# Attention kernel: the order of TensorE's instructions written out by hand, the other engines left to the scheduler

## The chip, the cores and the metric

The kernel runs on one core of a Trainium2 chip. The core has TensorE (PE, with its weight loads as PEld), VectorE (DVE), ScalarE (ACT), GpSimd (POOL) and a queue of transfers (SP); each works through its own instructions in order, and semaphores tie them together. The metric is the time of one execution in microseconds. Matmuls read on-chip memory (SBUF) and write accumulators (PSUM).

## The reference, cut to what matters

An attention whose mask allows only queries and keys of one cluster, followed by two expert layers. The attention, the part that changes:

```
B, H, S, D = 2, 8, 768, 64          # 16 heads, 16 clusters of each
q_assign = argmax(q_n @ c_n.T);  k_assign = argmax(k_n @ c_n.T)
mask = q_assign[:, :, :, None] == k_assign[:, :, None, :]
scores = where(mask, scale * q @ k.T, -1e9)
attn = softmax(scores);  out = attn @ v
...
x = moe(x)       # 1536 rows, 8 experts, with a skip
x = moe2(x)      # the same with an output gate
```

## The kernel before

**A head in six steps.** The 16 heads (`t`) are taken one after the other, and each in six steps (`i`) of 128 queries. `score` makes the 128x768 scores of a step in PSUM with four products: two with K and Q split in a high and a low part (`KA`, `QA`, 512 and 256 columns), two with `KB` and `QB` (L475, L477), whose last 16 rows hold the one-hot cluster of each token, so that the mask is added by the product. DVE takes the row maximum (`mx`, L481), ACT the exp with its sum (`probs`, L486). `flips` turns the 128x768 probabilities with six transpositions (L493) into two PSUM tiles `tp` of three each, which ACT and DVE copy to `PT`. There are two buffers for the scores, and two for `tp`. The code of a step first issues the score of the step after it, then the transpositions of its own.

**The products with V.** After three steps a half of the head (384 queries) is complete, and `av` multiplies it with V: six products (k = 0 to 5) of 64 x 384, the even ones into the upper 64 rows of one PSUM tile, the odd ones into the lower. In the trace each of them is two instructions (L505). `merge` then divides by the sums and multiplies with `G` (unit matrix and gate weights, L520).

**The work ahead.** In steps 3 to 5 of head `t`, `dots` makes the cluster products of head `t + 2`, four at a time, in the free quarter of the first `tp` tile of the step (L421); `dots_sum` adds them up on DVE (`dt`, L428), which frees that tile. Before L428 reads the tile, ACT must have copied its other part. `cluster` finds the cluster on DVE, `one_hot` transposes the result (L455, two products a head), and three transfers on SP bring it through memory into rows 64 to 79 of `QB` and `KB`. `load` and `split` fetch and split Q and K three and two heads ahead; `split` runs on POOL. In heads 1 to 8, `split_weights` splits a piece of expert weights, the high part on ACT (L136), the low part on DVE (L139); `behind` puts it behind the step's maximum and exp. From head 8 on `bg` runs the routing of the first batch a few instructions a step, its placing products at L263.

**What sets the order.** Through the attention the language's scheduler sets the order of each engine's instructions: it takes the program's order as a priority, and moves what it holds ready earlier. From the experts on, `tc.manual_schedule()` makes every engine issue in the order in which the code is written. There `tokens` runs the first expert's products with a list of events between them, which also finishes the last head.

Of the kernel before, what the change touches and what calls it, by code (L numbers as in the profile page):

```python
# [23 lines left out]
B, H, S, D = 2, 8, 768, 64  # L24
# [3 lines left out]
NJ = S // 128  # L28
# [12 lines left out]
def fused_kernel(ctx: ExitStack, tc: tile.TileContext, qT, kT, v, cN, wg, w11, w12, w21, w22, out):  # L41
# [17 lines left out]
    def iota_f(pool, name, n, pattern, base, cm):  # L59
        ti = pool.tile([128, n], I32, name=name + "i")  # L60
        nc.gpsimd.iota(ti, pattern=pattern, base=base, channel_multiplier=cm)
        tf = const.tile([128, n], F32, name=name)
        nc.gpsimd.tensor_copy(out=tf, in_=ti)
        return tf
# [102 lines left out]
    bg = Background()  # L167
# [163 lines left out]
    def route1(L, b, ps, pool, after=None, slack=6):  # L331
        do = pool.tile([128, NJ], F32, tag="do", name="do")
        nc.vector.tensor_scalar(out=do, in0=L[:, :, E], scalar1=0.0, scalar2=None, op0=ALU.is_gt)
        yield
        yield from route(L[:, :, 0:E], None, tok1[:, NJ * b:NJ * b + NJ], do, NJ, base1, TB1, ps, pool, after, slack)
# [23 lines left out]
    asm = pool("asm", 1, actx)  # L359
# [16 lines left out]
    def load(t):  # L376
        if t >= NH:
            return
        b, h = heads[t]
        qp = ld.tile([128, S], F32, tag="qp", name="qp")  # L380
        kp = ld.tile([128, S], F32, tag="kp", name="kp")
        vp = vpb.tile([128, NJ, D], F32, tag="vp", name="vp")
        for dst, src in ((kp, kT), (qp, qT)):
            for p in (LO, HI):
                nc.sync.dma_start(out=dst[p], in_=src[b, h])
        nc.sync.dma_start(out=vp, in_=v[b, :, h])
        raw[t] = (qp, kp, vp)

    def split(t):

        if t >= NH:
            return
        qp, kp, vp = raw.pop(t)
        QA = spl.tile([128, S], F32R, tag="QA", name="QA")
        KA = spl.tile([128, S], F32R, tag="KA", name="KA")
        QB = spl.tile([80, S], F32R, tag="QB", name="QB")
        KB = spl.tile([80, S], F32R, tag="KB", name="KB")
        if t == 0:
            nc.scalar.copy(out=KA[:], in_=kp)
            nc.vector.tensor_tensor(out=KA[HI], in0=kp[HI], in1=as32(KA[HI]), op=ALU.subtract)  # L400
            nc.scalar.activation(out=QA[:], in_=qp, func=AF.Copy, scale=SCALE)
            nc.vector.scalar_tensor_tensor(out=QA[LO], in0=qp[LO], scalar=SCALE, in1=as32(QA[LO]), op0=ALU.mult, op1=ALU.subtract)  # L402
        else:
            nc.gpsimd.tensor_scalar(out=KA[:], in0=kp, scalar1=1.0, scalar2=1.0, op0=ALU.mult, op1=ALU.mult)
            nc.gpsimd.tensor_tensor(out=KA[HI], in0=kp[HI], in1=as32(KA[HI]), op=ALU.subtract)
            nc.gpsimd.tensor_scalar(out=QA[:], in0=qp, scalar1=SCALE, scalar2=1.0, op0=ALU.mult, op1=ALU.mult)
            nc.gpsimd.tensor_scalar(out=qp[LO], in0=qp[LO], scalar1=SCALE, scalar2=1.0, op0=ALU.mult, op1=ALU.mult)
            nc.gpsimd.tensor_tensor(out=QA[LO], in0=qp[LO], in1=as32(QA[LO]), op=ALU.subtract)
        nc.sync.dma_start(out=as32(QB[LO]), in_=as32(QA[HI]))
        nc.sync.dma_start(out=as32(KB[LO]), in_=as32(KA[LO]))  # L410
        ops[t] = (QA, KA, QB, KB, vp)
# [18 lines left out]
    def cluster(t, n):  # L430
        if t >= NH:
            return
        for _ in range(n):
            next(clus[t][0])
# [60 lines left out]

    avp = {}

    def av(t, half, PT, k0, k1):
        vp = ops[t][4]
        if k0 == 0:  # L500
            avp[t] = ps_o.tile([128, 384], F32, tag="o", name="o")
        po = avp[t]
        for k in range(k0, k1):
            r = 64 * (k % 2)
            nc.tensor.matmul(out=po[r:r + 64, :], lhsT=vp[:, k, :], rhs=PT[:, k, :], start=(k < 2), stop=(k >= NJ - 2))  # L505
        if k1 == NJ:
            ot = asm.tile([128, 384], F32, tag="ot", name="ot", bufs=2)
            nc.scalar.copy(out=ot, in_=po)
            avp[t] = ot

    def merge(t, half):
        b, h = heads[t]
        ot = avp.pop(t)
        j0 = 3 * half
        rr = asm.tile([128, 3], F32, tag="rr", name="rr", bufs=2)
        nc.scalar.activation(out=rr, in_=sums[t][:, j0:j0 + 3], func=AF.Copy, bias=1e-9)
        nc.vector.reciprocal(out=rr, in_=rr)
        pf = ps_m.tile([128, 3, D + NG], F32, tag="misc", name="pf")
        for j in range(3):
            nc.tensor.matmul(out=pf[:, j], lhsT=ot[:, 128 * j:128 * j + 128], rhs=G[:, h], start=True, stop=True)  # L520
        if b not in xb:
            xb[b] = xp.tile([128, NJ, DM], F32, tag="xb", name="xb")
            lg[b] = (xp if b == 0 else const).tile([128, NJ, NG], F32, name=f"lg{b}")
        rb = rr.unsqueeze(2)
        x, L = xb[b][:, j0:j0 + 3], lg[b][:, j0:j0 + 3]
        if h == 0:
            nc.vector.tensor_tensor(out=L, in0=pf[:, :, D:], in1=rb.to_broadcast([128, 3, NG]), op=ALU.mult)
        else:
            lt = asm.tile([128, 3, NG], F32, tag="lt", name="lt", bufs=2)
            nc.vector.tensor_tensor(out=lt, in0=pf[:, :, D:], in1=rb.to_broadcast([128, 3, NG]), op=ALU.mult)  # L530
            (nc.vector if t == NH - 1 else nc.gpsimd).tensor_tensor(out=L, in0=L, in1=lt, op=ALU.add)
        nc.vector.tensor_tensor(out=x[:, :, D * h:D * h + D], in0=pf[:, :, 0:D], in1=rb.to_broadcast([128, 3, D]), op=ALU.mult)
        if h == H - 1:
            r0 = S * b + 384 * half
            for dst in (X, X2):
                nc.sync.dma_start(out=dst[r0:r0 + 384, :].rearrange("(j p) d -> p j d", p=128), in_=x)
# [43 lines left out]
    nc.vector.tensor_tensor(out=chl[:, :, 1], in0=c3, in1=as32(chl[:, :, 0]), op=ALU.subtract)  # L580

    split(0)
    d16 = iota_f(asm, "d16", NCL, [[-1, NCL]], NCL, 0)
    for c in (2, 1, 0):
        dp = ps_t.tile([128, 4, 128], F32, tag="tp", name="dp0")[:, 0].rearrange("p (t s) -> p t s", t=4)
        dots(0, c, dp)
        dots_sum(0, c, dp)
# [7 lines left out]
        nc.sync.dma_start(out=G[p, :, D:], in_=wg.rearrange("(h d) g -> d h g", d=D))  # L595
        nc.gpsimd.tensor_scalar(out=G[p, :, 0:D], in0=ident[p, p].unsqueeze(1).to_broadcast([64, H, D]), scalar1=1.0, scalar2=1.0, op0=ALU.mult, op1=ALU.mult)
    io128, io12, d8, tok1 = late_constants(asm)
    load(1)
    split(1)
    load(2)  # L600

    wsets = [w_tiles(wA, "A"), None]
    wdone = 0
    def flips(t, i, pr, hook=None, after=None):
# [15 lines left out]
    for c in range(3):  # L620
        dp = ps_t.tile([128, 4, 128], F32, tag="tp", name="dp1")[:, 0].rearrange("p (t s) -> p t s", t=4)
        dots(1, c, dp)
        dots_sum(1, c, dp)
    PT = {}
    for g, (t, i) in enumerate(steps[:-1]):
        half = i // 3
        if i % 3 == 0:
            PT[t, half] = ptb.tile([128, NJ, 384], F32, tag="PT", name="PT")
        old = pr
        cur = score(*steps[g + 1])  # L630
        pr = probs(*steps[g + 1], *cur)
        if i == 0:
            load(t + 3)
            split(t + 2)
            cluster(t + 1, 2)
        elif i == 1:
            if t:
                av(t - 1, 1, PT[t - 1, 1], 0, 6)
            cluster(t + 1, 2)
        elif i == 2:  # L640
            if t == NH - 1:
                first_turn()
            if t:
                merge(t - 1, 1)
                if t == H:
                    bg.add(route1(lg[0], 0, ps_m, asm, None, 2))
                    bg.add(first_tile())
                    bg.add(route_skip(lg[0], tok1[:, 0:NJ], ps_m, asm, 2))
            cluster(t + 1, 1)
            one_hot(t + 1)  # L650
        elif i == 3:
            if 1 <= t <= 8:
                if t == 1:
                    fetch(False, 2)
                behind(lambda: split_weights(t - 1, False, False))
        elif i == 4:
            behind(flush_late)
            av(t, 0, PT[t, 0], 0, 6)
        elif i == 5:
            merge(t, 0)  # L660

        dp = []

        def hook(tp):
            if i > 2 and t + 2 < NH:
                dp.append(tp[:, 3].rearrange("p (t s) -> p t s", t=4))
                dots(t + 2, i - 3, dp[0])

        def after(tp):
            if dp:  # L670
                dots_sum(t + 2, i - 3, dp[0])

        flips(t, i, old, hook, after)
        behind(lambda: bg.step(2))
    bg.drain()
    tl = NH - 1

# [375 lines left out]
    def first_of_batch1(L):  # L1053
# [29 lines left out]
    ht = h_tiles(128)  # L1083
    xg[0, 0] = rows_in(X[0:S], gi1[:, 0, 0:1])
    py = tokens(first, wsets[0], ht, half_of(0), events(
        (0, lambda: merge(tl, 0)), (18, last_probs), (26, lambda: av(tl, 1, PT[tl, 1], 0, 2)), (30, lambda: av(tl, 1, PT[tl, 1], 2, 6)),
        (36, last_merge), *plan(P['E0']), *steps(P['q4'], 72, 1)), (38, 43, 48, 54))
    flush()
    close_first(0, 0, 0, py)
# [209 lines left out]
```

## Time and profile before

| | us |
|---|---|
| median of 3 runs | 734.42 |
| lowest, highest | 728.52, 736.29 |
| the profiled execution | 733.56 |
| its span, first to last instruction | 731.8 |
| PE busy | 664.9 (91%) |
| DVE, ACT, POOL busy | 462.4, 401.2, 190.7 |
[...]

The attention ends, and the first expert product (L725) begins, at 314.75 us of the span; the rest belongs to the two expert layers. Starts of PE's instructions in a timeline tell its pace better than durations, since neighbouring matmuls overlap.

### The profile page before, as it was taken

The numbers are of one execution on the slowest core, as the hardware profiler recorded it, in microseconds if no ns is written. First come the engines' busy times: TensorE is split into PE (matmuls) and PEld (weight loads), VectorE is DVE, ScalarE is ACT, GpSimd is POOL, SyncE is SP. The second block draws the span as 40 slices with busy tenths as digits, with TensorE's granted clock in tenths as the row PEclk, the third lists the DMA queues.
The fourth block names the chain that finished last, engine by engine and source line by source line (L and its number), as shares of the span: only waits on it lengthen the run. The fifth ranks groups of instructions, "written<-read, shape, count | busy, mean of one in ns | idle before, by whom it ended". The sixth has DMA issues, their size and how long they took to land. (4 is left out here: it accounts for less than half of the span.)

```text
span 731.8 us, 11917 instructions
## 1 busy us (share of the span) xinstructions
PE 664.9 (91%) x4196; PEld 526.5 (72%) x4196; DVE 462.4 (63%) x964; ACT 401.2 (55%) x801; POOL 190.7 (26%) x193
## 2 busy tenths in 40 slices
PE   3889999999999999988888889789996999999995
PEld 2667666666667666767777778668885888899784
DVE  4546666667776676538768688657855755665620
ACT  2547666666565666644646666536634655555420
POOL 4614444444334330005202112202132022103011
PEclk9989999999999999998999899999999999999998
DMA  6665655556533110085737688637643576657200
GB/s 160 148 158 117 142 116 116 116 116 209 131 88 101 33 34 12 12 299 194 251 127 274 195 290 278 207 115 256 226 138 116 188 262 240 215 193 237 72 7 29
DMA packets 53034, 113.72 MB, mean 155 GB/s; under 512 B 7938, under 2 KB 15746, under 8 KB 52928
## 3 DMA queue, kind: packets, MB, share of 16 engines
q1 hardware_dynamic: 48016, 98.56, 44.8%
q0 software_dynamic: 4912, 13.88, 5.9%
q8 instruction: 51, 0.84, 0.5%
q14 instruction: 55, 0.45, 0.2%
HBM read 93.52 MB, written 14.71 MB: 148 GB/s over the span
## 5 line engine op out<-in xcount | busy, mean ns | idle before, releaser
L486 ACT ACTIVATE pr<-s,mx 128x768 f32<-128x768 f32 x96 | 86.8, 904 | 48.2 <-DVE mx L481 46.7
L481 DVE TENSOR_REDUCE mx<-s 128x1 f32<-128x768 f32 x96 | 90.9, 954 | 35.1 <-PE s L477 32.6
L493 PE MATMUL tp<-ident,pr 128*128 128x128 f32 x576 | 96.3, 291 | 2.9 <-ACT pr L486 2.7
L505 PE MATMUL o<-PT,vp 128*64 128x384 f32 x384 | 93.1, 499 | 0.6
L611 ACT COPY PT<-tp 128x384 f32<-128x384 f32 x144 | 67.0, 481 | 47.2 <-PE tp L493 28.5
L493 PEld LDWEIGHTS tp<-ident,pr 128*128 128x128 f32 x576 | 66.0, 146 | 35.9 <-ACT pr L486 12.5
L701 POOL DMA_INDIRECT xg<-x_rows,gi x33 | 40.2, 1217 | 112.2 <-PEq L1154 37.8
L475 PE MATMUL s<-KA,QA 128*128 128x512 f32 x192 | 64.8, 404 | 4.7 <-DVE QA L402 3.1
L725 PE MATMUL ph<-w1hA,xt 128*128 128x256 f32 x208 | 52.0, 313 | 8.7 <-DVEq L1154 5.2
L477 PE MATMUL s<-KB,QB 80*128 80x512 f32 x192 | 54.5, 369 | 1.1 <-ACT KB L445 1.1
L505 PEld LDWEIGHTS o<-PT,vp 128*64 128x64 f32 x384 | 29.8, 136 | 35.4 <-issue 30.4
L725 PE MATMUL ph<-w1hB,xt 128*128 128x256 f32 x192 | 46.2, 312 | 9.3 <-PEq L1154 4.2
L725 PE MATMUL py<-w2hA,hh 128*128 128x512 f32 x112 | 47.5, 424 | 4.1 <-DVE hh L799 4.1
L725 PE MATMUL py<-w2hB,hh 128*128 128x512 f32 x112 | 46.6, 417 | 3.5 <-DVE hh L799 3.5
L725 PEld LDWEIGHTS ph<-w1hA,xt 128*128 128x128 f32 x208 | 38.6, 204 | 12.8 <-issue 10.9
L725 PE MATMUL py<-w2lA,hh 128*128 128x512 f32 x112 | 47.1, 420 | 0.0
L725 PE MATMUL py<-w2lB,hh 128*128 128x512 f32 x112 | 46.3, 413 | 0.0
L613 DVE COPY PT<-tp 128x384 f32<-128x384 f32 x48 | 26.8, 557 | 29.1 <-PE tp L493 27.8
L725 PEld LDWEIGHTS ph<-w1hB,xt 128*128 128x128 f32 x192 | 35.5, 208 | 11.8 <-issue 10.2
L837 DVE SCALAR_TENSOR_TENSOR hl<-phw,hh 128x256 fp32r<-128x256 f32 x48 | 20.2, 421 | 36.0 <-ACT hh L836 36.0
L139 DVE TENSOR_TENSOR w1lA<-raw,w1hA 128x1024 fp32r<-128x1024 f32 x32 | 39.8, 1257 | 2.8 <-ACT w1hA L136 2.7
L136 ACT CAST w1hA<-raw 128x1024 fp32r<-128x1024 f32 x32 | 33.0, 1045 | 14.2 <-PEq L1154 6.2
(240 smaller groups left out, 1643.3 us busy)
## 6 DMA issues: line engine op xcount, KB each, us to landing
raw<-w SPq DMA_DIRECT2D x128, 512.0 KB, 4.9
kp<-kT SPq DMA_DIRECT2D x32, 192.0 KB, 4.6
qp<-qT SPq DMA_DIRECT2D x32, 192.0 KB, 4.6
x_rows<-xb SPq DMA_DIRECT2D x8, 768.0 KB, 5.7
vp<-v SPq DMA_DIRECT2D x16, 192.0 KB, 3.8
KB<-KA SPq DMA_DIRECT2D x16, 192.0 KB, 3.6
QB<-QA SPq DMA_DIRECT2D x16, 192.0 KB, 3.4
one_hot<-st SPq DMA_DIRECT2D x15, 96.0 KB, 1.7
```

Of the source, the lines that this page charges most:

```text
L136: nc.scalar.copy(out=hi, in_=src)
L139: nc.vector.tensor_tensor(out=lo, in0=src, in1=as32(hi), op=ALU.subtract)
L475: nc.tensor.matmul(out=s[:, n0:n1], lhsT=QA[:, sl], rhs=KA[:, n0:n1], start=True, stop=False)
L477: nc.tensor.matmul(out=s[:, n0:n1], lhsT=QB[:, sl], rhs=KB[:, n0:n1], start=False, stop=True)
L481: paced["DVE"] = nc.vector.tensor_reduce(out=mx, in_=s, axis=AX.X, op=ALU.max, negate=True).ins
L486: paced["ACT"] = nc.scalar.activation(out=pr, in_=s, func=AF.Exp, bias=mx, accum_out=sums[t][:, i:i + 1]).ins
L493: nc.tensor.transpose(out=tp[:, kk], in_=pr[:, 128 * k:128 * k + 128], identity=ident)
L505: nc.tensor.matmul(out=po[r:r + 64, :], lhsT=vp[:, k, :], rhs=PT[:, k, :], start=(k < 2), stop=(k >= NJ - 2))
L611: nc.scalar.copy(out=dst, in_=tp[:, 0:3])
L613: nc.vector.tensor_copy(out=dst, in_=tp[:, 0:3])
L701: nc.gpsimd.indirect_dma_start(out=xg, out_offset=None, in_=src, in_offset=bass.IndirectOffsetOnAxis(ap=gi, axis=0))
L725: nc.tensor.matmul(**kw)
```

## The change

PE alone is taken out of the scheduler's hands for the loop over heads: `tc.manual_schedule(engines={PE})`. The loop's body is written in the order wanted of PE: the score of the next step, then the six products of a half (in steps 0 and 3), the transpositions with the dots, and then the merge (after steps 1 and 4) or the one-hot pair (after step 2). The products of a head's second half move from step 1 of the next head to its step 0, those of the first half from step 4 to step 3. The merge of the last head's first half stands in the loop instead of in the experts' events. Ahead of the loop, the loads of heads 1 and 2 and the split of head 1 stand earlier. The number of instructions is the same.

```diff
     split(0)
+    load(1)
+    split(1)
     d16 = iota_f(asm, "d16", NCL, [[-1, NCL]], NCL, 0)
+    load(2)
...
-    load(1)
-    split(1)
-    load(2)
...
+    order = ExitStack()
+    order.enter_context(tc.manual_schedule(engines={mybir.EngineType.PE}))
     for g, (t, i) in enumerate(steps[:-1]):
...
         if i == 0:
+            if t:
+                av(t - 1, 1, PT[t - 1, 1], 0, 6)
             load(t + 3)
             split(t + 2)
-            cluster(t + 1, 2)
+            cluster(t + 1, 3)
         elif i == 1:
-            if t:
-                av(t - 1, 1, PT[t - 1, 1], 0, 6)
             cluster(t + 1, 2)
         elif i == 2:
             if t == NH - 1:
                 first_turn()
+        elif i == 3:
+            av(t, 0, PT[t, 0], 0, 6)
+            if 1 <= t <= 8:
...
+        elif i == 4:
+            behind(flush_late)
...
+        flips(t, i, old, hook, after)
+        if i == 1:
             if t:
                 merge(t - 1, 1)
...
-            cluster(t + 1, 1)
+        elif i == 2:
             one_hot(t + 1)
-        elif i == 3:
...
         elif i == 4:
-            behind(flush_late)
-            av(t, 0, PT[t, 0], 0, 6)
-        elif i == 5:
             merge(t, 0)
...
-        flips(t, i, old, hook, after)
         behind(lambda: bg.step(2))
+    order.close()
...
     py = tokens(first, wsets[0], ht, half_of(0), events(
-        (0, lambda: merge(tl, 0)), (18, last_probs), (26, lambda: av(tl, 1, PT[tl, 1], 0, 2)), (30, lambda: av(tl, 1, PT[tl, 1], 2, 6)),
+        (18, last_probs), (26, lambda: av(tl, 1, PT[tl, 1], 0, 2)), (30, lambda: av(tl, 1, PT[tl, 1], 2, 6)),
```

PE in steps 3 and 4 of an early head, before (`o` is the PSUM tile of the products with V, `tp` that of the transpositions and of the dots, `s` that of the scores):

```order
L505 MATMUL o<-PT,vp 64x384
L493 MATMUL tp<-ident,pr 128x128 x3
L421 MATMUL tp<-chl,QA 128x32 x4
L493 MATMUL tp<-ident,pr 128x128 x3
L475 MATMUL s<-KA,QA 128x512
L475 MATMUL s<-KA,QA 128x256
L477 MATMUL s<-KB,QB 128x512
L477 MATMUL s<-KB,QB 128x256
L505 MATMUL o<-PT,vp 64x384 x5
L493 MATMUL tp<-ident,pr 128x128 x3
```

The same place after:

```order
L505 MATMUL o<-PT,vp 64x384 x6
L493 MATMUL tp<-ident,pr 128x128 x3
L421 MATMUL tp<-chl,QA 128x32 x4
L493 MATMUL tp<-ident,pr 128x128 x3
L475 MATMUL s<-KA,QA 128x512
L475 MATMUL s<-KA,QA 128x256
L477 MATMUL s<-KB,QB 128x512
L477 MATMUL s<-KB,QB 128x256
L493 MATMUL tp<-ident,pr 128x128 x3
```

One of the six products stood ahead of the transpositions of step 3 and five behind the score of step 5; now all six stand ahead, and the transpositions of step 4 follow the score directly.

DVE at the same place, before (`mx` are the maxima of steps 4 and 5, `dt` the sums of the dots of steps 3 and 4, `w2lA` the low part of a piece of weights):

```order
L481 TENSOR_REDUCE mx_1467<-s_1462 128x1
L613 COPY PT_1461<-tp_1484 128x3x128
L481 TENSOR_REDUCE mx_1494<-s_1489 128x1
L139 TENSOR_TENSOR w2lA_268<-raw_1071,w2hA_267 128x1024
L428 TENSOR_REDUCE dt_1480<-tp_1472 128x64
L428 TENSOR_REDUCE dt_1480<-tp_1510 128x64
```

And after:

```order
L481 TENSOR_REDUCE mx_1469<-s_1464 128x1
L612 COPY PT_1463<-tp_1495 128x3x128
L481 TENSOR_REDUCE mx_1505<-s_1500 128x1
L428 TENSOR_REDUCE dt_1491<-tp_1483 128x64
L139 TENSOR_TENSOR w2lA_268<-raw_1082,w2hA_267 128x1024
L428 TENSOR_REDUCE dt_1491<-tp_1512 128x64
```

The sum of step 3's dots still stands behind the maximum of step 5, and the piece of weights has moved behind that sum. In a head that splits no weights DVE's order after is another:

```order
L481 TENSOR_REDUCE mx_2829<-s_2824 128x1
L199 TENSOR_TENSOR geq_2821<-geq_2821,d8_259 128x48
L202 TENSOR_REDUCE gwm_2860<-geq_2821 128x6
L612 COPY PT_2823<-tp_2854 128x3x128
L428 TENSOR_REDUCE dt_2850<-tp_2842 128x64
L481 TENSOR_REDUCE mx_2867<-s_2862 128x1
```

There the sum (`dt_2850`) has moved ahead of the maximum of step 5 (`mx_2867`).

## Rows read from the trace of the kernel before

**Rows 1.** Windows by engine, steady part: window, length, busy us (instructions), clock, DMA.

```profile
core 0: us, PE busy (x) PEld busy (x) DVE busy (x) ACT busy (x) POOL busy (x), PEclk, DMA share, GB/s
100.00:140.00 40.00, 39.84 (x245) 26.59 (x241) 27.72 (x55) 27.27 (x63) 15.13 (x14) 1.00 0.57 130
```

**Rows 2.** Waits of PE, 22 to 315 us: total us, times, longest.

```profile
PE tp L493 <- ACT pr L486: 2.7, 4, 1.7
```

**Rows 3.** Timeline of PE within one head: start, length, instruction, count.

```profile
107.10 0.28 PE L455 MATMUL po<-identb,oh 128*96 128x128 bf16 x2
...
107.48 0.86 PE L505 MATMUL o<-PT,vp 128*64 128x384 f32 x2
108.27 0.55 PE L493 MATMUL tp<-ident,pr 128*128 128x128 f32 x3
...
109.32 0.60 PE L475 MATMUL s<-KA,QA 128*128 128x512 f32 x2
...
110.19 2.15 PE L505 MATMUL o<-PT,vp 128*64 128x384 f32 x10
112.27 0.55 PE L493 MATMUL tp<-ident,pr 128*128 128x128 f32 x3
```

**Rows 4.** Timeline of PE: the one-hot pairs of five heads, as marks.

```profile
32.67 0.28 PE L455 MATMUL po<-identb,oh 128*96 128x128 bf16 x2
...
71.21 0.28 PE L455 MATMUL po<-identb,oh 128*96 128x128 bf16 x2
...
125.03 0.28 PE L455 MATMUL po<-identb,oh 128*96 128x128 bf16 x2
...
199.50 0.28 PE L455 MATMUL po<-identb,oh 128*96 128x128 bf16 x2
...
291.51 0.28 PE L455 MATMUL po<-identb,oh 128*96 128x128 bf16 x2
```

**Rows 5.** Timeline of PE at the end of the attention.

```profile
298.93 1.55 PE L263 MATMUL pt<-grhs,gop 128*128 128x96 f32 x12
...
303.21 0.88 PE L493 MATMUL tp<-ident,pr 128*128 128x128 f32 x6
303.84 0.59 PE L475 MATMUL s<-KA,QA 128*128 128x512 f32 x2
...
311.28 2.16 PE L505 MATMUL o<-PT,vp 128*64 128x384 f32 x12
313.37 0.88 PE L493 MATMUL tp<-ident,pr 128*128 128x128 f32 x6
...
314.75 0.36 PE L725 MATMUL ph<-w1hA,xt 128*128 128x256 f32 x1
```

**Rows 6.** Timeline of all engines: score, maximum, exp, transpositions.

```profile
102.94 0.51 PE L477 MATMUL s<-KB,QB 80*128 80x512 f32 x2
...
103.50 0.96 DVE L481 TENSOR_REDUCE mx<-s 128x1 f32<-128x768 f32 x1 [0.67 <-PE s L477]
...
104.75 0.91 ACT L486 ACTIVATE pr<-s,mx 128x768 f32<-128x768 f32 x1
...
105.80 0.87 PE L493 MATMUL tp<-ident,pr 128*128 128x128 f32 x6
```

**Rows 7.** Groups of DVE, 60 to 300 us: busy us, mean ns.

```profile
L428 DVE TENSOR_REDUCE dt<-tp 128x64 f32<-128x128 f32 x38 | 10.7, 283 | 11.3 <-ACT PT L611 11.3
```

**Rows 8.** Timeline of SP's queue: the last one-hot transfer of a head.

```profile
128.16 0.42 SPq L461 DMA_DIRECT2D KB<-one_hot  x1
```

**Rows 9.** Tile KB, 60 to 300 us: transfers from issue to landing.

```profile
DMA to landing us min/median/max: 2.0/3.0/6.8
```

**Rows 10.** Windows of PE: window, length, busy us, clock, DMA.

```profile
46.46:53.29 6.83, 5.95 (x24) 0.50 0.83 233
...
343.50:352.00 8.50, 5.92 (x47) 1.00 0.87 304
```

**Rows 11.** Timeline of PE: two starts after a pause.

```profile
47.34 1.54 PE L493 MATMUL tp<-ident,pr 128*128 128x128 f32 x6 [1.72 <-ACT pr L486]
...
345.76 0.34 PE L741 MATMUL tp<-ident,hs 128*128 128x128 f32 x1 [1.24 <-DVE hs L817]
```

More of the change, by code (lines that the diff above doesn't have):

```diff
@@ L496, in fused_kernel, with av @@
     avp = {}
-    def av(t, half, PT, k0, k1):
+    def av(t, half, PT, n0, n1):
         vp = ops[t][4]
-        if k0 == 0:
+        if n0 == 0:
             avp[t] = ps_o.tile([128, 384], F32, tag="o", name="o")
         po = avp[t]
-        for k in range(k0, k1):
+        for k in range(n0, n1):
             r = 64 * (k % 2)
             nc.tensor.matmul(out=po[r:r + 64, :], lhsT=vp[:, k, :], rhs=PT[:, k, :], start=(k < 2), stop=(k >= NJ - 2))
-        if k1 == NJ:
+        if n1 == NJ:
             ot = asm.tile([128, 384], F32, tag="ot", name="ot", bufs=2)
@@ L642, in fused_kernel @@
                 first_turn()
[L643 to L648, printed above, removed]
-            cluster(t + 1, 1)
-            one_hot(t + 1)
         elif i == 3:
+            av(t, 0, PT[t, 0], 0, 6)
             if 1 <= t <= 8:
@@ L657, in fused_kernel @@
             behind(flush_late)
-            av(t, 0, PT[t, 0], 0, 6)
-        elif i == 5:
-            merge(t, 0)
         dp = []
@@ L673, in fused_kernel @@
         flips(t, i, old, hook, after)
+        if i == 1:
+            if t:
+                merge(t - 1, 1)
+                if t == H:
+                    bg.add(route1(lg[0], 0, ps_m, asm, None, 2))
+                    bg.add(first_tile())
+                    bg.add(route_skip(lg[0], tok1[:, 0:NJ], ps_m, asm, 2))
+        elif i == 2:
+            one_hot(t + 1)
+        elif i == 4:
+            merge(t, 0)
         behind(lambda: bg.step(2))
+    order.close()
     bg.drain()
```

## The prediction

> **What bounds the kernel now.** I read the windows by engine first, then the waits of TensorE (PE), then its timeline head by head, and last the groups of VectorE (DVE). In the steady part of the attention PE is busy 39.84 of 40.00 us at the full clock [rows 1], and its longest kind of wait over the whole attention comes to 2.7 us in four pieces [rows 2]; for 60 to 190 us the view of waits names none at all. ScalarE (ACT) and DVE stand at 27 to 28 of 40 us in the same window. So here a microsecond taken out of PE's own stream is a microsecond of the kernel, until another engine's chain comes up behind it. One head lasts 125.03 - 107.10 = 17.93 us, measured from the two one-hot products of one head to those of the next [rows 3, 4].
>
> PE's stream is not at its floor. The six products of a half (12 instructions, since each runs in two passes) stand split: two instructions from 107.48 to 108.27 (0.79 us), and ten more from 110.19 to 112.27 (2.08 us), together 2.87 us. Where all twelve stand in one run, they go from 311.28 to 313.37, 2.09 us [rows 3, 5]. The two column halves of the array work side by side, so ten cost what twelve do, and the lone product costs 0.78 us. It is split in that way in 27 of 32 halves.
>
> **The change part by part.**
>
> *Six products in one run.* Two halves a head: 2 x 0.78 = 1.56 us off PE's stream. The rest of the written order costs, from rows where each unit stands whole: a score 0.87 (109.32 to 110.19) [rows 3]; six transpositions 0.63 (303.21 to 303.84), and with a merge behind them 1.38 (313.37 to 314.75), so a merge 0.75 [rows 5]; transpositions with the four dot products between them 1.05 (108.27 to 109.32) [rows 3]; the one-hot pair about 0.1. A head has six scores (5.22), two runs of products (4.18), three plain sets of transpositions (1.89), three with dots (3.15), two merges (1.50) and the pair: 16.0 us if PE never waits, 1.9 less than now. The score is taken where a run of products follows; elsewhere it looks nearer 0.80, so this sum may be 0.3 too high.
>
> *A cover that goes.* The order of now is: one product, transpositions of step 3, score of step 5, the other five products, transpositions of step 4. The order after is: all six, transpositions of step 3, score of step 5, transpositions of step 4. These last need the buffer that step 3 filled, which DVE frees when it has summed the dot products. In the heads that split weights DVE takes the row maximum of step 5 ahead of that sum, before and after. So PE ends the score, the maximum starts 0.05 after the score's end (103.45 to 103.50) and takes 0.96, the sum takes 0.28, and with the score's own tail (0.1) and the handoff PE waits about 1.4 us [rows 6, 7]. Now 2.08 us of products lie over this; after the change nothing does. It is paid in heads 1 to 8. In head 0 and from head 9 on DVE's new order has the sum ahead of the maximum; the sum must then only wait for ACT's copy of the same tile, and I take 0.3.
>
> *The loop of scores, maximum, exp and transpositions.* A score's transpositions may start 0.05 + 0.96 after its end plus 1.05 from exp's start to the transpositions (104.75 to 105.80) [rows 6], about 2.1 in all. The next score always stands ahead of them, and with it products (2.09), a merge (0.75) or dots. The thinnest place is step 2: transpositions and merge 1.38, score 0.87, together 2.25. That covers it by a hair; I take 0.1 a head for it and for the run of products that opens a head, whose last copy stands behind a maximum on DVE. In the late heads exp of step 5 stands behind two copies: 0.2 more. Bounds for these small waits: 0 and 1 us a head.
>
> So a head with weights takes 16.0 + 1.4 + 0.1 = 17.5 us, and one without 16.0 + 0.3 + 0.1 + 0.2 = 16.6.
>
> *One-hot rows.* The pair now stands after the transpositions of step 2. Behind it on SP's queue go three DMAs whose landing the second half of the next head's first score waits for. The record issues the last of them 128.16 - 125.03 = 3.1 us after the pair, and they land after 3.0 us in the median, 6.8 at worst [rows 4, 8, 9]. The new order needs them 0.87 + 2.09 + 1.05 + 0.87 + 1.05 + 0.75 us after the pair, and half a score (0.4) later still: 7.1, or 8.5 with the wait. I take no cost; the bound is 3 us in a late head.
>
> *Loads moved up.* The loads and the split of head 1 stand ahead of the loads of G on SP's queue. G is wanted only by the first merge, near 38 us, and the split is wanted by the dots. I take 1 us gained before the first mark; bounds -2 and +2.
>
> *Merge of the last head's first half.* It leaves the expert's events, but it stood directly ahead of the first expert product there too (between 313.37 and 314.75) [rows 5]; nothing moves. The expert part keeps its order: 0, with 4 us either way.
>
> **The sum**, from mark to mark [rows 4]. To 32.67: 1 gained. From there to 71.21, two heads in 38.5; after, 16.6 + 17.5 = 34.1: 4.4 gained (part of it is the stretch at half clock from 46.46 to 53.29 [rows 10], which need not come back). To 199.50, seven heads in 128.3; after, 7 x 17.5 = 122.5, and 2 for the first products and waits of routing: 3.8 gained. To 291.51, five heads in 92.0; after, 5 x 16.6 = 83.0, two sets of 12 placing products at 1.55 [rows 5], 3.1, and 1 of waits: 4.9 gained. From the run of products after this mark to 314.75 the order has three times score, six products and transpositions (3 x 3.59), three times score, transpositions and merge (3 x 2.25), two lone steps (1.5, and 1.9 with four turns of the first tile), 12 placing products (1.55) and 0.5 of waits, less the first score, which stood ahead of the mark: 22.1 against 23.0, 0.9 gained. Together 15.0 us. The profiled execution took 733.56 us (span 731.8), 0.9 under the median of the runs shown: **733.56 - 15.0 = 719 us.**
>
> **The rivals.**
>
> *The wait of 1.4 us does not show, and the scores cost 0.80.* DVE's order is fixed, but the maximum could end sooner after the score than I count. For it: the score is the unit that I counted high. Against: DVE works in order, and the sum stands behind the maximum in all eight heads. Price: 8 x 1.4 + 16 x 0.3 = 16 us less, 703 us.
>
> *PE was not the bound.* If the split products only filled time in which PE would have waited for exp, a head stays near 17.9, and only the start and the end gain: about 730 us. For it: the scheduler put pieces where it saw room. Against: not one wait of PE between 60 and 190 us.
>
> *The clock answers to the new pauses, briefly.* [...] If each brought a fall half as long as the one shown, 3.4 us, half of that is lost: 8 x 1.7 = 13.7 more, 733 us.
>
> *The clock answers for longer: slower than now.* If each pause brought a fall as long as the one that the rows show, 6.83 us, a head loses 3.4 us, more than the products give it: 719 + 27 = 746 us. It turns the sign at five falls and is slower by 1% from seven on. For it: that row. Against: the row of 343.5 to 352.
>
> [...]
>
> **How the numbers follow.** Forecast 0.62, the missing wait 0.14, PE not the bound 0.08, short falls 0.10, long falls 0.06. The range reaches from 705 (most of the missing wait and of the smaller scores) to 731 (the two cases near 730), and leaves the ends out: 0.8. A change of 1% (7.3 us) is about what a measurement of this kernel can tell from none. Faster by more than that: the forecast and the missing wait, 0.76, and a part of the cases near 730, 0.79 in all; within it 0.15; slower 0.06.
>
> **What would show it.** In the profile after: runs of twelve L505 products of 2.1 us in every head; marks 17.5 apart up to the ninth head and 16.6 to 17.5 after it, where routing adds its products; one wait of PE of about 1.2 to 1.4 us a head before transpositions, put down to DVE's sum of the dots (L428), in the early heads alone; the first expert product near 300 us instead of 314.75; the expert part as long as now, 417 us. I am wrong if the marks stay 17.9 apart, if the granted clock shows half in most heads, or if waits on exp come up in steps 1 to 3, which I priced at 0.1.

## The result and the profile after

The changed kernel takes 704.44 us (median of four runs, 702.09 to 707.77) against 732.69 for the kernel before: a ratio of 0.9615, 95% interval 0.957 to 0.966. That is clearly faster, and 0.6 us below the low end of the range (705); the forecast was 719. The profiled execution took 706.17 us, its span is 704.5. TensorE (PE) is busy 27 us less, as the first part of its profile page says:

```profile
PE 637.5 (90%) x4196; PEld 517.1 (73%) x4196; DVE 466.4 (66%) x964; ACT 401.2 (57%) x801; POOL 191.9 (27%) x193
```

The windows of PE, and its waits from 22 to 310 us, which answer to [rows 1, 2]:

```profile
100.00:140.00 40.00, 38.82 (x270) 28.70 (x270) 31.73 (x62) 28.48 (x67) 22.27 (x20) 1.00 0.59 133
```

```profile
PE tp L493 <- DVE dt L428: 2.7, 8, 0.3
PE s L477 <- DMA KB<-one_hot: 2.2, 1, 2.2
...
PE tp L493 <- ACT pr L486: 1.0, 1, 1.0
```

In the same 40 us PE now does 270 instructions where it did 245, still at the full clock. The forecast wait before transpositions, on VectorE's (DVE's) sum of the dots, is there in eight heads as predicted; but it is 0.34 us long, not 1.4. The timeline of one head, around step 4, shows why:

```profile
95.75 2.16 PE L505 MATMUL o<-PT,vp 128*64 128x384 f32 x12
...
99.17 0.56 DVE L612 COPY PT<-tp 128x384 f32<-128x384 f32 x1 [2.36 <-PE tp L493]
...
99.32 0.51 PE L477 MATMUL s<-KB,QB 80*128 80x512 f32 x2
...
99.87 0.96 DVE L481 TENSOR_REDUCE mx<-s 128x1 f32<-128x768 f32 x1
99.88 0.52 PE L493 MATMUL tp<-ident,pr 128*128 128x128 f32 x3
...
100.15 0.38 PE L421 MATMUL tp<-chl,QA 128*128 128x32 f32 x2
...
100.75 0.28 DVE L428 TENSOR_REDUCE dt<-tp 128x64 f32<-128x128 f32 x1
...
101.08 0.55 PE L493 MATMUL tp<-ident,pr 128*128 128x128 f32 x3 [0.34 <-DVE dt L428]
101.47 0.80 PE L520 MATMUL pf<-G,ot 128*128 128x89 f32 x6
102.06 0.61 PE L475 MATMUL s<-KA,QA 128*128 128x512 f32 x2
```

The twelve instructions of a half stand in one run, as planned. The first three transpositions of step 4 start at 99.88, while the maximum still runs and the sum of step 3's dots (100.75 to 101.03) has not begun: they do not wait for it. By this timing they go into the buffer that DVE's copy (99.17 to 99.73) has just freed; the names in the trace do not tell buffers apart, and the experiment with tied buffers below tests it. Only the second three take the buffer of the dots, and by then 0.86 us of transpositions and dots (99.88 to 100.74) lie over the wait.

The marks (the one-hot pairs, as [rows 4]), from the timeline of PE:

```profile
29.43 0.28 PE L455 MATMUL po<-identb,oh 128*96 128x128 bf16 x2
...
62.06 0.28 PE L455 MATMUL po<-identb,oh 128*96 128x128 bf16 x2
...
160.28 0.28 PE L455 MATMUL po<-identb,oh 128*96 128x128 bf16 x2
...
182.42 0.27 PE L455 MATMUL po<-identb,oh 128*96 128x128 bf16 x2
...
267.45 0.28 PE L455 MATMUL po<-identb,oh 128*96 128x128 bf16 x2
```

From 45.68 to 160.28 they are 16.37 us apart (17.93 before), then one gap is 22.14 (160.28 to 182.42), and the five behind it are 16.2 to 17.9. Against the forecast:

| stretch | gain forecast | gain measured |
|---|---|---|
| to the first mark | 1.0 | 32.67 - 29.43 = 3.2 |
| two heads | 4.4 | 38.5 - 32.6 = 5.9 |
| seven heads | 3.8 | 128.3 - 120.4 = 7.9 |
| five heads | 4.9 | 92.0 - 85.0 = 7.0 |
| to the first expert product | 0.9 | 23.2 - 24.3 = -1.0 |
| the experts, to the span's end | 0 | 417.1 - 412.8 = 4.3 |
| sum | 15.0 | 27.3 |

The long gap holds one transfer that came late. SP's queue, and PE at its end:

```profile
159.43 0.90 SPq L536 DMA_DIRECT2D x_rows<-xb  x2
162.25 0.32 SPq L459 DMA_DIRECT2D one_hot<-st  x1
```

```profile
167.99 0.33 SPq L461 DMA_DIRECT2D QB<-one_hot  x1
168.37 0.42 SPq L461 DMA_DIRECT2D KB<-one_hot  x1
```

```profile
170.39 1.01 PE L477 MATMUL s<-KB,QB 80*128 80x512 f32 x2 [2.24 <-DMA KB<-one_hot]
```

```profile
169.99:176.82 6.83, 6.43 (x24) 4.60 (x26) 3.96 (x9) 2.36 (x5) 2.16 (x2) 0.50 0.76 200
```

Two stores of the first batch's rows stand ahead of the one-hot rows of that head. PE waits 2.24 us, and the granted clock stands at half (0.50) for 6.83 us: this gap is 5.8 us longer than the one before it (the routing's first products stand in it too).

### The profile page after: what moved, and what is told of

Same layout as the page of the kernel before. It is cut to its first block, busy times and chain, and to the rows that moved or that the text cites. A ratio compares the mean times of both kernels' runs of the same rounds, so it can differ in the third digit from the quotient of the medians.

```text
span 704.5 us, 11900 instructions
## 1 busy us (share of the span) xinstructions
PE 637.5 (90%) x4196; PEld 517.1 (73%) x4196; DVE 466.4 (66%) x964; ACT 401.2 (57%) x801; POOL 191.9 (27%) x193
## 5 line engine op out<-in xcount | busy, mean ns | idle before, releaser
L493 PE MATMUL tp<-ident,pr 128*128 128x128 f32 x576 | 93.0, 286 | 5.3 <-DVE dt L428 2.7
L493 PEld LDWEIGHTS tp<-ident,pr 128*128 128x128 f32 x576 | 63.6, 143 | 36.6 <-ACT pr L486 22.4
L505 PE MATMUL o<-PT,vp 128*64 128x384 f32 x384 | 71.4, 501 | 0.6 <-ACT PT L610 0.6
L475 PE MATMUL s<-KA,QA 128*128 128x512 f32 x192 | 59.1, 388 | 3.3 <-DVE QA L402 3.3
L477 PE MATMUL s<-KB,QB 80*128 80x512 f32 x192 | 51.2, 350 | 3.3 <-DMA KB<-one_hot 2.2
L729 PE MATMUL ph<-w1hB,xt 128*128 128x256 f32 x192 | 43.7, 299 | 7.9 <-PEq L1212 2.1
L505 PEld LDWEIGHTS o<-PT,vp 128*64 128x64 f32 x384 | 25.9, 138 | 32.2 <-issue 26.3
L729 PEld LDWEIGHTS ph<-w1hA,xt 128*128 128x128 f32 x208 | 38.5, 203 | 10.6 <-issue 7.6
L729 PEld LDWEIGHTS ph<-w1hB,xt 128*128 128x128 f32 x192 | 33.4, 196 | 10.5 <-issue 8.8
L339 DVE TENSOR_TENSOR xt<-tp,xt 128x512 fp32r<-128x512 f32 (+1 forms) x32 | 21.7, 679 | 29.0 <-ACT xt L338 27.1
L840 ACT ACTIVATE hh<-phw 128x256 fp32r<-128x256 f32 x48 | 18.4, 384 | 38.4 <-PE phw L729 37.2
```

The costliest lines, as they stand in the source:

```text
L339: nc.vector.tensor_tensor(out=lo, in0=tp, in1=as32(hi), op=ALU.subtract)
L475: nc.tensor.matmul(out=s[:, n0:n1], lhsT=QA[:, sl], rhs=KA[:, n0:n1], start=True, stop=False)
L477: nc.tensor.matmul(out=s[:, n0:n1], lhsT=QB[:, sl], rhs=KB[:, n0:n1], start=False, stop=True)
L493: nc.tensor.transpose(out=tp[:, kk], in_=pr[:, 128 * k:128 * k + 128], identity=ident)
L729: nc.tensor.matmul(**kw)
```

## The experiments

**The products split again, in the written order.**

```diff
         if i == 0:
             if t:
-                av(t - 1, 1, PT[t - 1, 1], 0, 6)
+                av(t - 1, 1, PT[t - 1, 1], 0, 1)
...
         elif i == 1:
+            if t:
+                av(t - 1, 1, PT[t - 1, 1], 1, 6)
...
         elif i == 3:
-            av(t, 0, PT[t, 0], 0, 6)
+            av(t, 0, PT[t, 0], 0, 1)
...
         elif i == 4:
             behind(flush_late)
+            av(t, 0, PT[t, 0], 1, 6)
...
```

> The written order is kept, but the six products of a half stand split again, one in steps 0 and 3 and five in steps 1 and 4, with the merges where they stood before (the second half's ahead of the transpositions of step 2). Theory A, the gain is the products in one run: each split costs 0.78 us again, 1.56 a head, less the 0.34 us wait on the sum of the dots, which five products now cover; marks 17.2 to 17.6 apart in the early heads, 704.4 + 16 x 1.56 - 8 x 0.34 = 727 us (722 to 731). Theory B, the gain is the written order as such (scores whole, merges and one-hot pairs in set places): marks stay within 0.3 of 16.4, and the time stays below 711 us.

Measured: 728.63 us, 0.9941 of before (0.9913 to 0.997), marks 17.57 apart. Theory A holds in the marks. The timeline of PE in this kernel:

```profile
101.47 0.86 PE L505 MATMUL o<-PT,vp 128*64 128x384 f32 x2
102.25 0.55 PE L493 MATMUL tp<-ident,pr 128*128 128x128 f32 x3
...
104.18 2.15 PE L505 MATMUL o<-PT,vp 128*64 128x384 f32 x10
106.26 0.55 PE L493 MATMUL tp<-ident,pr 128*128 128x128 f32 x3
```

The lone product takes 0.78 us and the other five 2.08, as in [rows 3]. Of the 17.94 - 16.37 = 1.57 us a head that the change gave, the split takes back 1.2 (two lone products, 1.56, less the wait of 0.34 that the five products cover again). What is left, 17.94 - 17.57 = 0.37, I put down to the scores and transpositions that stand whole; no run tests that alone. That the time meets theory A's 727 so closely is in part luck: in the profiled execution the attention ends 17.8 us later than in the changed kernel (309.52 against 291.72), where theory A's sum has 22, and the span grows by another 7.8 us in the experts, which hold 20.5 us at half clock short of the end where the changed kernel's hold 13.7.

**The whole run where the five products stood.** The six products go to steps 1 and 4, with the merges where they were in the kernel above (`av(..., 0, 6)` there, nothing in steps 0 and 3).

> The six products stay in one run, but stand where the five stood before: behind the score of steps 1 and 4, with nothing ahead of steps 0 and 3. Theory A, PE's stream sets the time and products also cover the chain score, maximum, exp: the wait on the sum of the dots (0.34 us in eight heads) goes, but between the score of step 3 and its transpositions only 1.6 us of other work is left where the chain takes 2.1, and 1.9 at step 0, so new waits on exp of 0.5 and 0.2 us a head: marks 16.6 to 16.9, 707 to 713 us. Rival, where the run stands makes no difference: marks 16.0, 702 us.

Measured: 715.82 us, ratio 0.976 (0.9699 to 0.9821), marks 16.44 to 16.61 apart in the steady heads: above the rival's 16.0, at or below theory A's 16.6 to 16.9; the time is above both. Its waits of PE from 60 to 160 us:

```profile
PE tp L493 <- ACT pr L486: 2.2, 6, 0.4
PE po L455 <- DVE xb L532: 1.0, 6, 0.2
```

The wait on exp comes once a head, 0.37 us at step 0; the 0.5 that I had put on step 3 does not show. So where the run stands is worth 0.15 us in a steady head. The 11.5 us between the two spans lie elsewhere: 3.3 in the first three gaps, where one-hot rows come late by 1.07 and 0.70 us, 1.8 in the ninth (late by 3.86, with a fall of the clock), 2.9 in the five late gaps, and 4.0 in the experts, with 20.5 us at half clock there, short of the end, where the changed kernel has 13.7; from the last mark to the experts it is 1.3 us shorter.

**Buffers tied to their tile.** This makes the wait that was predicted:

```diff
-    ps_t = pool("ps_t", 2, actx, space=PSUM)
+    ps_t = pool("ps_t", 1, actx, space=PSUM)
...
-        tp = ps_t.tile([128, 4, 128], F32, tag="tp", name="tp")
+        tp = ps_t.tile([128, 4, 128], F32, tag=f"tp{c}", name="tp")
...
```

> The two buffers of the transpositions are tied to the first and the second tile of a step, so that step 4's first tile must take the buffer that step 3's dots were in. Theory A, the prediction failed because step 4's first tile takes the other buffer: with tied buffers the wait that was predicted comes, 1.2 to 1.4 us a head before the first transpositions of step 4 in heads 1 to 8, in place of 0.34 before the second three; 8 x 1.0 = 8 us more, 713 us, marks 17.4 in the early heads. Rival, the maximum and the sum were mis-sized and end soon enough anyway: marks stay near 16.4, 704 us. If a pause of 1.3 us a head brings the clock down: 3.4 us at half clock in each gives 727 us, 6.8 us in each 740 us.

Measured: 712.85 us, ratio 0.9701 (0.963 to 0.9772), marks 17.12 apart. Its timeline at step 4, and its windows:

```profile
103.05 0.96 DVE L481 TENSOR_REDUCE mx<-s 128x1 f32<-128x768 f32 x1
...
103.92 0.28 DVE L428 TENSOR_REDUCE dt<-tp 128x64 f32<-128x128 f32 x1
...
104.26 0.55 PE L493 MATMUL tp<-ident,pr 128*128 128x128 f32 x3 [1.25 <-DVE dt L428]
```

```profile
50.00:160.00 110.00, 101.00 (x707) 75.71 (x705) 77.93 (x155) 76.84 (x178) 50.95 (x47) 1.00 0.54 123
```

The wait is 1.25 us in each of eight heads and stands before the first three, as theory A has it: the maximum and the sum were sized nearly right (1.4), the buffer was wrong. The marks grow by 0.75 us, not by the 0.91 that the wait grows by, and stay below theory A's 17.4. The attention ends 6.1 us later than in the changed kernel (297.79 against 291.72), 5.2 of it in seven of these heads. That the medians differ by 8.4 us, as theory A's 8 has it, is partly chance: their intervals overlap. And the pauses do not bring the clock down: it stays at the full level through seven of them.

**The changed text, PE left to the scheduler.** The line that takes PE out of its hands is removed.

> The text of the changed kernel, but with PE left to the scheduler like the other engines. It then keeps the six products together in 26 of 31 halves of the loop, but still breaks scores and merges up. Theory A, the gain is the products in one run: five splits of 0.78 us come back (4 us), and switches between broken-up scores cost up to 0.35 us a head (5 us): 708 to 714 us. Theory B, the written order as such: marks near 17.9 again, 725 us or more.

Measured: 718.36 us, ratio 0.9805 (0.9753 to 0.9857): between the two. In the early heads theory A holds: marks 16.51 apart with the products whole. Three pauses of PE stand in the other heads:

```profile
45.67 0.95 PE L493 MATMUL tp<-ident,pr 128*128 128x128 f32 x6 [1.72 <-ACT pr L486]
```

```profile
182.75 1.48 PE L493 MATMUL tp<-ident,pr 128*128 128x128 f32 x6 [2.69 <-ACT pr L486]
```

```profile
232.82 0.52 PE L493 MATMUL tp<-ident,pr 128*128 128x128 f32 x3 [1.63 <-DVE lt L530]
```

A fall of the clock lies at each (3.41, 3.41 and 6.83 us at half), and the heads around them are 24.36, 21.02 and 21.89 us long. The first is the pause that the kernel before shows [rows 11]. The attention ends 13.8 us later than in the changed kernel (305.48 against 291.72): 6.3 of it lie in the first two gaps and 5.4 in the head of the third pause; the head of the second is 1.1 us shorter than in the changed kernel, which has its own pause there. So the order of the text gives about half of the whole gain (733.05 to 718.36), through the scheduler, and the written order the other half, for the most part in the heads where PE then does not run out of cover.

**A merge over the wait that is left.**

```diff
         def after(tp):
             if dp:
                 dots_sum(t + 2, i - 3, dp[0])
+            if i == 4:
+                merge(t, 0)
...
         elif i == 2:
             one_hot(t + 1)
-        elif i == 4:
-            merge(t, 0)
```

> The merge of a head's first half stands between the two tiles of step 4 instead of behind them. Theory A: its 0.6 to 0.75 us of PE work then lies over the wait of 0.34 us on the sum of the dots; marks 16.03 apart in the early heads instead of 16.37, 8 x 0.34 = 2.7 us less, 702 us. Rival, the wait only moves, since the merge waits for ScalarE's copy of the products, or the second three copies come too late for the next score: marks 16.3 or more, 704 us.

Measured: 701.73 us (699.25 to 705.24), marks 16.16 apart.

```profile
99.73 0.88 PE L520 MATMUL pf<-G,ot 128*128 128x89 f32 x6
99.88 0.28 DVE L428 TENSOR_REDUCE dt<-tp 128x64 f32<-128x128 f32 x1
...
100.45 0.49 PE L493 MATMUL tp<-ident,pr 128*128 128x128 f32 x3
```

The merge runs while DVE finishes the maximum and the sum, and no wait is named before the second three. The gain is 0.2 us a head instead of 0.34, and 0.3 to 0.7 in the late heads, which neither theory had. The 2.7 us between the medians lie within the spread of the runs.

**The loads where they were.** `load(1)`, `split(1)` and `load(2)` go back behind the loads of G.

> The loads of heads 1 and 2 and the split of head 1 stand where they did before, behind the loads of G; the rest is the changed kernel. Theory A, the 3.2 us by which the first mark came earlier are the early loads' own: the first mark returns from 29.4 to 31.5 to 32.7, and the time is 2 to 3 us above the changed kernel's, 707 us. Rival, they come from PE's written order: the first mark stays near 29.4 and the time at 704.4 us.

Measured: 704.27 us (700.04 to 709.86), first mark at 28.92, third at 61.55 (62.06 in the changed kernel). The first mark and the time are the rival's: in this kernel the early loads gave nothing (the last experiment shows another case). The rest of the rival, that the earlier mark comes from PE's written order, does not follow: PE left to the scheduler, with the early loads, has its first mark at 28.26, so PE need not be held to the order for it. In this profile the one-hot rows came late by only 1.01 us, and the clock did not fall:

```profile
168.65 0.62 PE L477 MATMUL s<-KB,QB 80*128 80x512 f32 x2 [1.01 <-DMA KB<-one_hot]
```

**The two stores behind the one-hot rows.** The two stores of head 7's second half are issued after the last one-hot transfer that head 8 makes (for head 9), instead of in `merge`.

> In the changed kernel PE waits once for 2.24 us, in the head whose one-hot rows stand on the queue behind two stores of the first batch's rows, and the clock stands at half for 6.83 us from 169.99 on. Here those two stores (and no others) stand behind that head's one-hot transfers. Theory A, the stores delay the one-hot rows and the pause brings the clock down: the wait and the fall both go, that head is 22.13 - 2.24 - 3.4 = 16.5 us long, and the time is 5.6 us less, 699 us. Rival, the rows are late for another reason (the queue behind the loads of Q): the wait stays, 704 us.

Measured: 704.56 us (702.73 to 705.53). SP's queue and PE's windows in this kernel:

```profile
162.88 0.33 SPq L459 DMA_DIRECT2D one_hot<-st  x1
...
164.64 0.31 SPq L461 DMA_DIRECT2D QB<-one_hot  x1
165.00 0.42 SPq L461 DMA_DIRECT2D KB<-one_hot  x1
165.52 0.91 SPq L684 DMA_DIRECT2D x_rows<-xb  x2
```

```profile
160.00:290.00 130.00, 125.57 (x875) 93.44 (x874) 97.19 (x236) 86.60 (x210) 38.32 (x41) 1.00 0.27 76
```

The rows follow in 1.8 us instead of 5.7, wait and fall are gone, and the gap is 17.74 instead of 22.14 us. The edit moves one transfer more: the load of Q that the changed kernel issues between the one-hot transfers, at 162.66, comes at 156.54 here. The kernel with the whole run late tells the two apart: there the load of Q is out of the way (158.93), the stores stand ahead (164.30), and the rows follow after 7.0 us (165.97 to 172.96). So the stores are enough to make the rows late. But the median has not moved. So both kernels were run once more, side by side:

> The changed kernel a second time, beside the one whose two stores stand behind the one-hot rows, to see where the 4.4 us went that the head of the stores gave up and the medians do not show. Theory A, the pause before the one-hot rows differs from run to run (2.24 us here, 1.01 us with other loads), and with it the fall of the clock: the times spread from 700 to 708 us about 703.5, and this profile shows a pause of another size in that head. Rival, pause and fall come each time: 2 to 2.5 us and a fall of 3.4 to 6.8 us again, 704 to 706 us.

> The two stores behind the one-hot rows, a second time, on the same chip as the changed kernel. Theory A: no pause over 1 us in the head of the stores, times that spread less (701 to 706 us) and a median 1 to 3 us below the changed kernel's. Rival, what the head gains the experts' part gives back in falls of the clock: median within 0.7 us of the changed kernel's.

Measured: the changed kernel 706.61 us (703.14 to 708.96), with the same pause of 2.24 us and the same fall of 6.83; the other 705.94 (701.39 to 707.92). Theory A falls in both: the pause came the same in both profiles. The attention ends at 291.72 and 292.53 in the changed kernel, at 287.98 and 287.65 with the stores moved; the experts then take 412.8 and 414.3 against 413.0 and 417.2. The windows of the experts' part with the stores moved, first and second time:

```profile
287.98:701.00 413.02, 369.98 (x2395) 318.17 (x2395) 255.05 (x504) 210.91 (x356) 74.19 (x64) 0.97 0.59 195
```

```profile
287.65:704.90 417.25, 371.21 (x2395) 318.81 (x2395) 255.47 (x504) 210.62 (x356) 77.01 (x64) 0.97 0.59 193
```

By the granted clock these parts hold 22.6 and 25.5 us at half clock, the changed kernel's 19.0 and 17.1: half of the differences, 1.8 and 4.2 us, is given back there. What stays are spans of 701.0 against 704.5 us and 704.9 against 706.8. All runs together agree, since the granted clock of each is on record: its mean is 0.983 over ten runs of either kernel, and the mean times are 704.8 us with the stores moved and 705.9 without. So about as much time goes at half clock as before, although the profiles no longer show the 6.83 us in the attention. Why the experts then hold more of it, whether because they begin 4 us earlier or for another reason, stays open.

**Both together, and all three.** The merge over the wait and the two stores; then the late loads as well.

> The merge between the tiles of step 4 and the two stores behind the one-hot rows, together. If both theories hold, 2.7 + 5.6 us less than the changed kernel: 696 us (692 to 700), marks 16.03 apart up to the ninth head. If the parts don't add up, because a shorter head brings the one-hot rows or the exp late, 699 us or more.

> The merge between the tiles of step 4, the two stores behind the one-hot rows, and the loads of heads 1 and 2 where they stood before. The late loads alone brought the first mark 0.5 us earlier. If the parts add up: 699 us (696 to 701). If the loads matter only by chance of the transfers: no difference from 699.5 us.

Measured: 699.47 us (698.88 to 704.86), 0.9558 of before (0.9521 to 0.9595), and 701.73 us (699.16 to 705.25), 0.9576 (0.9546 to 0.9606). The first has the lowest median of the study, 5 us under the changed kernel's; the parts do not add up to 696, as the stores alone gave nothing in the median. The late loads do not help here: with them PE pauses for 2.23 us until 29.99, a fall of 3.41 us lies there, and the first mark is at 31.32 instead of 29.03. The ranges of the two kernels overlap.

## Why the prediction was wrong, by its steps

**Six products in one run: right.** PE's sum for a head was 16.0 us. Measured: 16.37 - 0.34 = 16.03; with tied buffers 17.12 - 1.25 = 15.87, and 16.16 in the kernel that names no wait. The closeness is in part luck, as the units' errors cancel. In the head from 94.88 to 111.25 of the changed kernel six scores take 5.29 us (5.22 counted), two merges 1.18 (1.50), three plain sets of transpositions 2.00 (1.89), and three with dots, without the wait, 3.31 (3.15). The lone product's 0.78 us came back in the first experiment. The starts of the instructions show where it comes from, first in the split half of the kernel before, then in a whole run of the changed kernel:

```profile
107.48 0.54 PE L505 MATMUL o<-PT,vp 128*64 128x384 f32 x1
...
107.85 0.49 PE L505 MATMUL o<-PT,vp 128*64 128x384 f32 x1
...
111.85 0.49 PE L505 MATMUL o<-PT,vp 128*64 128x384 f32 x1
```

```profile
95.75 0.54 PE L505 MATMUL o<-PT,vp 128*64 128x384 f32 x2
...
96.12 0.49 PE L505 MATMUL o<-PT,vp 128*64 128x384 f32 x2
```

In the whole run the instructions start two at a time, the second pair 0.37 us after the first. Those of the lone product start singly, also 0.37 us apart, and so does the last of the ten others, at 111.85. So two products run side by side where they stand together, and a lone one takes as long as two: the two instructions take 0.78 us, and the ten 2.08, as twelve do.

**A cover that goes: the step that failed.** It said that the transpositions of step 4 "need the buffer that step 3 filled, which DVE frees when it has summed the dot products", and priced 1.4 us in eight heads. Only the second three need it. At step 4 the first tile gets the buffer that came free first, the one which DVE copied, not the one that waits for the sum. Seven heads took 16.37 instead of 17.5, and the eighth lost 0.34 instead of 1.4: 9 us, three quarters of the 12.3 us by which the spans miss the sum. With this step right the sum gives 719 - 9 = 710 us, inside the range. The other 3.3 us are what is left of errors of both signs: 2.2 to the first mark, 0.3 in the next head, 2.1 in the five late heads and 4.3 in the experts came out shorter; 3.7 in the rest of the head of the stores and 1.9 at the end came out longer. With tied buffers the kernel takes 712.85 us, which the range held. The order shown ahead of the prediction could not tell it, as its names leave out which buffer a tile got, and I took it that the first tile of a step always has the first buffer.

**Loops of score, maximum, exp: right.** After the first mark no wait on exp shows in steps 1 to 3; one of 1.01 us stands in step 2 of head 0, until 28.72. The late heads, without their placing products (two sets of 1.33 us), take 16.5 a head; 16.6 was forecast.

**One-hot rows: mis-sized.** I took no cost, with a bound of 3 us. It came to 2.24 us of wait and, by estimate, 3.4 for the clock (half of 6.83), in the one head where two stores stand ahead on the queue; the run with the stores moved puts both together at 4.4 (22.14 to 17.74), with another pause of 0.84 us in their place. The row from which I took the 3.1 us between the pair and the last transfer [rows 8] was of a head without stores. The kernel before has the head with stores in its own trace, and there the last transfer is issued 8.7 us after the pair (178.86):

```profile
178.44 0.90 SPq L536 DMA_DIRECT2D x_rows<-xb  x2
179.87 0.58 SPq L459 DMA_DIRECT2D one_hot<-st  x1
...
187.52 0.42 SPq L461 DMA_DIRECT2D KB<-one_hot  x1
```

Read from this head, the sum would have had a wait in it.

**Loads moved up: cause not borne out.** The first three marks gained 9.1 us where 5.4 was forecast. Put back alone, the loads took nothing away (704.27 us); put back in the kernel with all three, they came with a first mark 2.3 us later. What they are worth, and what brought the first mark forward by 3.2 us, stays open. The forecast left open whether the stretch at half clock [rows 10] comes back; the written order took out the pause of 1.72 us, which the scheduler brings back with the same text, and with it the fall, by estimate 3.4 us.

**The last heads: mis-sized.** From the last mark on I counted 0.5 us of waits; three rows show 0.74, 0.58 and 0.88:

```profile
274.11 1.55 PE L263 MATMUL pt<-grhs,gop 128*128 128x96 f32 x12 [0.74 <-DVE xb L532]
...
285.89 2.16 PE L505 MATMUL o<-PT,vp 128*64 128x384 f32 x12 [0.58 <-ACT PT L610]
...
291.72 0.39 PE L729 MATMUL ph<-w1hA,xt 128*128 128x256 f32 x1 [0.88 <-ACT pr L486]
```

**The experts: 0, and 4.3 measured**, beyond the 4 of the bound. Of it 3.4 is the clock, if half of the time at half clock counts: short of the end, 20.5 us at half before and 13.7 after. The order in that part is the same in all kernels of the study, and their profiles hold from 10.2 to 20.5 us at half in it, short of the end, so a pair of profiles can differ by this much without the change. The granted clock of all runs says that some of it is no chance: its mean is 0.978 over the 34 runs of the kernel before that stand beside the experiments and 0.983 over the ten of the changed one, which makes 32 and 24 us at half. The profiles put 10.24 and 6.83 of that in the attention, so some 5 us less at half, in the mean, are the experts', if the attention is alike in every run. What in the change brings that about is not shown.

**The rivals.** "The wait does not show, and the scores cost less" had nearly the right time (703) and the wrong half of its reason: the wait mostly went, but the six scores of a head cost what was counted, 5.29 us (0.78 to 0.99 each). PE was the bound. Neither clock rival came: with waits of 1.25 us in eight heads, as tied buffers make them, seven brought no fall at all. One such pause every 17.12 us left the granted clock at the full level (1.00) from 50 to 160 us.

## What to carry to other kernels

Before pricing a wait on a buffer, find out which buffer the tile gets, at each step: where a pool hands out what is free first, one late reader shifts the turn of all that follow. Where one engine is the bound, count its stream unit by unit from rows where each unit stands whole; that sum held within 0.2 us a head, with single terms off by up to 0.3. Then walk through every queue of a head that is not like the others (stores, routing), and read its delays from that same head, since a written order waits there for whatever comes late.

## What the runs showed of the hardware

Pauses of PE inside the attention, from 28 us on and ahead of the last head (all of 1 us and more, and some that are shorter), and the stretch at half clock that belongs to them (it began at most 2.4 us before and 1.9 us after the pause's end):

| kernel | pause, us (its end) | at half clock, us |
|---|---|---|
| tied buffers | 1.25, seven times (52.90 to 155.63) | none |
| tied buffers | 1.25 and 1.39 (172.75, 176.46) | 3.41 |
| stores moved, twice | 0.84, 0.85 (174.74, 174.44) | none |
| late loads | 1.01 (168.65) | none |
| changed kernel; merge over the wait; stores moved | 1.01, 1.16, 1.09 (28.72, 28.77, 28.67) | none |
| whole run late | 1.21, 1.07 (28.80, 38.21) | none |
| all three | 2.23 (29.99) | 3.41 |
| before | 1.72 (47.34) | 6.83 |
| before | 0.82 and 0.56 (191.82, 192.73) | 3.41 |
| PE left to the scheduler | 1.72 (45.67), 2.69 (182.75), 1.63 (232.82) | 3.41, 3.41, 6.83 |
| changed kernel, twice | 2.24 (170.39, 171.10) | 6.83, 6.83 |
| split again | 1.97 (180.87) | 6.83 |
| merge over the wait | 2.74 (168.69) | 3.41 |
| whole run late | 3.86 (175.49) | 10.24 |

Beside a pause of the same length (1.72 us) stood 3.41 us once and 6.83 another time, and beside a longer one (2.74) less than beside a shorter one (2.24): 3.41 against 6.83. So one such pause with a fall cost, by estimate (half of the time at half clock), 1.7 to 3.4 us on top of itself, five for the longest, and its price can't be read from its length. The experts' part differs by the run in the same way: 413.0 and 417.2 us in two profiles of the kernel with the stores moved, with 22.6 and 25.5 us at half clock.
